# A paired feed-forward on one Trainium2 core: second products taken one token tile at a time in two PSUM banks, attention scores made three tiles at a time in six

## The chip, the cores and the metric

The kernel runs on one core of one Trainium2 chip. The metric is the device time of one execution in microseconds (us). The engines have short names here, as in the profile: PE is TensorE, the matrix unit, and PEld its weight loads; DVE is VectorE, ACT is ScalarE, POOL is GpSimd, and SP only issues DMAs. Each engine works through its own instructions in the order in which the program emits them, and waits on semaphores where another engine has to be done first. PSUM, where PE leaves its results, has eight banks of 512 fp32 columns.

## The reference

Grouped attention over 8 samples of 384 tokens (16 query heads, 4 key heads, 64 columns a head), and then a feed-forward block on its output `x` (384 x 1024 per sample):

```
scores = q @ k^T / 8 ; attn = softmax(scores) ; x = attn @ v
a1  = alpha1 * x + beta1
u   = x + lam * (w_tok @ a1)            # mixes tokens, 384 x 384
a2  = alpha2 * u + beta2
out = u + lam * (relu(a2 @ w_ch1) @ w_ch2)   # 1024 -> 4096 -> 1024
```

## The kernel before, in words

**Samples.** Samples 0 and 1 go through a plain feed-forward (`main`). Samples 2 to 7 go in three pairs (`pair(i)`, samples 2+2i and 3+2i), and a pair's two large products are done with seven block products in place of eight; the sums that this needs are made by DVE. Attention for later samples is woven between the feed-forward matmuls: `main(0)` carries sample 1, `main(1)` carries 2 and 3, the second phase of pair 0 carries samples 4 and 5, that of pair 1 carries 6 and 7, and pair 2 carries none.

**A pair has two phases.** In the first (L693 to L738) PE makes the hidden layer: 8 groups of 14 blocks, each of 4 matmuls on 384 columns, into tiles that the code calls X, Y and Z. In the second (L739 to L796) it makes the output: seven products `o`, in the order 1, 2, 6, 5, 3, 7, 4, each of 3 token tiles `ms` by 16 hidden tiles `t`, so 48 matmuls on 512 columns into tiles called C. The 16 are cut in two halves `h`, and the three token tiles take turns within a half: three banks stay open. Sums over products are left to PSUM: a product that starts anew has `start` at its first matmul (only 1, 6 and 7), and the next products add to what lies there. After a half with h = 1 a C tile is evacuated: a copy by ACT (product 1), an add by DVE (6, 5, 3, 7, 4) or a multiplication by lam (2). For 3, 7 and 4 a multiplication by lam follows through `flush`, and a store by a POOL DMA.

**Units.** The generator stops (`yield`) every 4 second-product matmuls. One such step is called a unit here; a product has 12 and the phase has 84, numbered from 0. A table says what of attention is emitted after which unit (`put` at L450 and L932, `put_all(ps, 1, side(c)[1])` at L969 for the pair's first sample, and the same with 36 added for its second, L972). The entries per sample are:

- S, a block of scores: `scores2` (L303) makes two tiles of 1024 scores each, by 4 matmuls with 64 rows a tile, and ACT turns each tile to exponentials (L289). 18 tiles make a sample, so there are nine blocks, at units 0, 4, 8, ... 32.
- A (`av`, L410): 18 matmuls of attention times v for two heads; then DVE does a reciprocal, a multiplication that frees the PSUM tile (L328) and two operations for a1 (L333, L335). At units 7, 11, ... 35.
- T (`tok`, L341): 9 matmuls with w_tok; then DVE adds (L352), which frees the tile, and multiplies (L356), which makes a2. At units 10, 14, ... 38. Two units later a2 is spilled and turned by a DMA transpose (`flip`).
- turn (L429), only for head pairs 5 to 7 of the pair's second sample: PE transposes a2 instead, in 3 matmuls. At units 33, 36 and 40, so with 36 added 69, 72 and 76, each 2 units or more after its T.

**Other DVE work of the second phase.** `sums_a` (L590, 3 small operations each) at units 75, 75, 76 and 78 combines a2 for the next pair; `sum_w1` (L622) at the start of three (h, ms) blocks of product 4; and four "hidden sums" in each of products 2 and 6 (L788 to L794) of 0.95 us.

**PSUM in the pairs.** Pool `sc` gives tiles of two banks, two of them in turn: S, T and turn take one each, and so do the Y tiles. Pool `acc` gives three single banks: X, every second Z, and C. Pool `one` is a single bank: A and the other Z. A new tile of a pool takes the place of the oldest, and its first matmul waits until the last reader of that one is done.

**Weights of the second products** come as 28 blocks of 512 KB per pair, fetched by SP into a ring of 6 slots that the first-phase weights use too. `free` (L645) gives a slot back after its last matmul and starts one more load of the queue. The last two blocks of a pair go to `pad`, where there is room for two.

Of the kernel before, what the change touches and what calls it, by code (L numbers as in the profile page):

```python
# [12 lines left out]
def kernel(  # L13
# [182 lines left out]
    def three():  # L196
        if pairs:
            return pairs["sc"].tile([P, 2, 4, P], f32, tag="sc", name="sc", bufs=2)
        return threes[0].tile([P, 2, 4, P], f32, tag="sc", name="sc", bufs=3)

    def one():
        if pairs:
            return pairs["one"].tile([P, 4, P], f32, tag="one", name="one", bufs=1)
        return three()[:, 0]
# [25 lines left out]
    def side(b):  # L230
# [71 lines left out]

        def scores2(i):  # L303
            for k in range(2):
                scores(2 * i + k)
# [130 lines left out]
        if not first:  # L436


            turns = {}
            if b == 1:  # L440
                turns = {4: [(to_all, 3, 0, 0), (to_all, 3, 1, 1), (load_row_set, 1, 1, 0), (load_row_set, 2, 0, 1)],
                         8: [(k_transpose, 0)], 12: [(to_all, 1, 0, 2), (to_all, 1, 1, 0), (load_row_set, 2, 1, 0)],
                         16: [(scale_beta,)], 20: [(to_all, 2, 0, 1), (to_all, 2, 1, 0)],
                         24: [(q_transpose, 0, 2, "av")], 28: [(k_transpose, 2)]}
                for i in range(3):
                    turns[32 + 4 * i] = [(q_transpose, 2 + 2 * i, 2, "av")]
            if (b - NPL) // 2 > 0:
                at = {}

                def put(k, *m):  # L450
                    at.setdefault(k, []).append(m)

                for j in range(9):
                    put(4 * j, scores2, j)
                for p in range(NP):
                    put(4 * (p + 1) + 3, av, p)
                    put(4 * (p + 1) + 6, tok, p)
                    put(4 * (p + 1) + 8, flip, p)
                    if by_pe(p):
                        put(4 * (p + 1) + 8 + (p == NP - 3), turn, p)  # L460
                return turns, at
            return turns, {
                0: [(scores3, 0)], 4: [(av, 0)], 6: [(scores3, 1)], 8: [(tok_flip, 0)], 11: [(av, 1)],
                13: [(scores3, 2, True)], 15: [(av, 2)], 16: [(tok_flip, 1)], 18: [(tok_flip, 2)], 19: [(av, 3)],
                21: [(scores3, 3)], 23: [(tok_flip, 3)], 25: [(av, 4)], 27: [(scores3, 4)], 29: [(tok_flip, 4)],
                31: [(av, 5)], 33: [(scores3, 5, True)], 35: [(av, 6), (tok_flip, 5)], 37: [(av, 7)],
                38: [(tok_flip, 6)], 41: [(tok_flip, 7)],
                **{39 + 4 * i - i // 2 * 2: [(turn, p)] for i, p in enumerate((5, 6, 7)) if by_pe(p)}}
# [167 lines left out]
    def fetch(i, n, at=None):  # L636
        if at is None:
            w2_slots[i, n] = w1_free.pop(0)
            at = ring[:, w2_slots[i, n]]
        else:  # L640
            w2_slots[i, n] = None
        w2_at[i, n] = at
        nc.sync.dma_start(out=at, in_=w2s[n])

    def free(slot):  # L645
        if slot is None:
            return
        w1_free.append(slot)
        if queue:
            f, *a = queue.pop(0)  # L650
            f(*a)

    queue = [m for i in range(NB) for m in [(load_w1, c) for c in order1[2 if i else RING:]]
             + [(fetch, i, n) for n in range(SLOTS - 2 if i + 1 < NB else SLOTS)] + [(load_w1, c) for c in order1[:2] if i + 1 < NB]]
# [6 lines left out]
    def pair(i):  # L661
# [5 lines left out]
        def begin_end(ms):  # L667
            ends[ms] = t = piece().bitcast(f32)
            nc.sync.dma_start(out=t, in_=by_tok(out[b0 + 1])[:, ms, :512])
# [5 lines left out]
        def scaled(o, b, ms, dw, t):  # L675
            if o != 2:
                tt(out=t, in0=t, in1=lam_t[:, dw * 512:(dw + 1) * 512], op=MUL)  # L677
            store(b, ms, dw, t)
# [9 lines left out]

        def finish(ts):
# [3 lines left out]
        for g in range(NH // 2):  # L693
            X, Y, snap = {}, {}, {}
            for k, (o, e) in enumerate(SEQ1):
                t = 2 * g + e
                lo, hi = bias1[:, t:t + 1], bias1[:, NH + t:NH + t + 1]
                if o == 1:
                    X[e] = acc.tile([P, 512], f32, tag="acc", name="X", bufs=3)
                if o == 7:  # L700
                    Y[e] = pairs["sc"].tile([P, 2, 512], f32, tag="sc", name="Y", bufs=2)[:, 0]
                if o == 2:
                    Z = acc.tile([P, 512], f32, tag="acc", name="Z", bufs=3) if e else pairs["one"].tile(
                        [P, 512], f32, tag="one", name="Z", bufs=1)
# [35 lines left out]
        X = [[(0, 512, acc.tile([P, 512], f32, tag="acc", name="C", bufs=3))] for _ in range(NST)]  # L740
        snap = {}
        where = {2: (0, 0), 3: (0, 1), 7: (1, 1), 4: (1, 0)}
        for k, o in enumerate(PLACE2):
            for h in range(2):
                for ms in range(NST):
                    if o == 4 and not last and 1 < 3 * h + ms < 5:
                        sum_w1(0, (5, 7, 6)[3 * h + ms - 2])
                    if o == 5 and not last and h and ms < 2:
                        fetch(i, SLOTS - 2 + ms, pad[:, (1 + ms) * 2048:(2 + ms) * 2048])
                    if last and (o, h) in ((6, 1), (7, 0)):  # L750
                        (lift_end if o == 7 else begin_end)(ms)
                    if last and (o, h, ms) == (7, 0, NST - 1):
                        X[ms] = [(c0, c1, pairs["sc"].tile([P, 2, 512], f32, tag="sc", name="C", bufs=2)[:, 0, :c1 - c0])
                                 for c0, c1 in ((0, 384), (384, 512))]
                    for (c0, c1, x), t in ((c, t) for c in X[ms] for t in range(8 * h, 8 * h + 8)):
# [3 lines left out]
                                         start=(o in (1, 6, 7) and t == 0), stop=(t == NH - 1), skip_group_check=True)  # L759
                        if t % 4 == 3 and ms == NST - 1 and c1 == 512:  # L760
                            free(slot)
# [5 lines left out]
                        if t % 8 == 3 and c1 == 512:  # L767
                            flush(1)
                            yield 1
                    if h == 1 and not (last and o == 4):  # L770
# [6 lines left out]
                        for c0, c1, x in X[ms]:  # L777
                            if o == 1:
                                nc.scalar.copy(out=snap[o, ms], in_=x)
                            elif o in (6, 5):  # L780
                                tt(out=snap[o, ms], in0=x, in1=snap[1, ms], op=ADD)
                            elif o == 2:
                                tt(out=t, in0=x, in1=lam_t[:, :512], op=MUL)
                            else:
                                tt(out=t[:, c0:c1], in0=x, in1=snap[{3: 1, 7: 5, 4: 6}[o], ms][:, c0:c1], op=ADD)
                        if o not in (1, 6, 5):
                            later.append((scaled, o, b0 + bb, ms, dw, t))
                    if o in (2, 6) and (h, ms) in ((0, 1), (0, 2), (1, 0), (1, 1)):  # L788
                        r = [(0, 1), (0, 2), (1, 0), (1, 1)].index((h, ms))
                        ts = slice(4 * r, 4 * r + 4)  # L790
                        if o == 2:
                            tt(out=hid[:, ts, 0], in0=hid[:, ts, 3], in1=hid[:, ts, 0], op=SUB)
                        else:
                            tt(out=hid[:, ts, 4], in0=hid[:, ts, 4], in1=hid[:, ts, 0], op=SUB)  # L794
# [5 lines left out]
    with tc.manual_schedule(engines=order):  # L800
# [162 lines left out]
        for i in range(NB - 1):  # L963
# [6 lines left out]
            for u, f, h in ((10, flip_q, 0), (17, flip_k, 0), (18, flip_q, 2), (25, flip_q, 4), (33, flip_k, 2), (33, flip_q, 6)):  # L970
                put(ps, 1, u, f, c + 1, h, 2)
            put_all(ps, 1, side(c + 1)[1], lambda u: u + 36)  # L972
            for j, u in ((1, 75), (0, 75), (2, 76), (3, 78)):
                put(ps, 1, u, sums_a, j)
        for ps in range(NPL + NB):
# [8 lines left out]
            if ps == NPL - 1:  # L984
                side_banks.close()
                mm_banks.close()
                for name in ("sc", "acc", "one"):
# [33 lines left out]
```

## Time and profile before

| what | us |
|---|---|
| three runs | 743.80, 743.89, 745.25 (median 743.89) |
| the profiled execution, its own time | 745.27 |
| its span, first to last instruction | 743.5 |
| PE idle before an instruction, longest: at the very start, then anywhere later | 1.52, 0.60 |

By stage (the view of busy time by stretch), in us; the two second phases that carry attention are in the fourth and sixth row:

| stretch | length | PE busy | DVE busy | ACT busy |
|---|---|---|---|---|
| `main(1)`, first phase, 130.9 to 190.1 | 59.2 | 57.46 | 40.94 | 22.34 |
| `main(1)`, second phase, to 244.2 | 54.1 | 53.48 | 38.24 | 18.78 |
| pair 0, first phase, to 316.9 | 72.7 | 72.70 | 63.10 | 48.38 |
| pair 0, second phase, to 418.9 | 102.0 | 101.05 | 74.91 | 38.33 |
| pair 1, first phase, to 491.8 | 72.9 | 72.90 | 56.38 | 48.42 |
| pair 1, second phase, to 593.7 | 101.9 | 100.95 | 74.82 | 38.28 |
| pair 2, first phase, to 666.7 | 73.0 | 73.00 | 56.00 | 48.47 |
| pair 2, second phase and end, to 743.5 | 76.8 | 72.42 | 31.76 | 2.11 |

How to read it: a line of the timeline has the start, the time from the start of its first instruction to the end of its last, the engine, the line of the code, the operation, `out<-in` by tile names, the shape, and how many instructions were merged; a bracket at the end is the idle time of that engine ahead of it and what ended it. Matmuls overlap, so the time that a block takes on PE is read from start to start of two blocks, not from its length. A few matmul records are missing from the trace: where a group shows x7 or x3, it had 8 or 4.

### The profile page before, as it was taken

The page shows a single profiled execution, that of the slowest core. Times are in us where ns is not written, and L with a number is a line of the kernel's source. Part 1 is how long each engine was busy: PE and PEld are TensorE (multiplying, and loading weights), DVE is VectorE, ACT ScalarE, POOL GpSimd, SP SyncE. Part 2 cuts the span into 40 slices and gives each one's busy share as a digit, 9 for nine tenths or more (in the row PEclk, how much of TensorE's full clock was granted, in tenths as well). Part 3 has the DMA queues.
Part 4 walks back from the last instruction along what each step waited for, and adds up shares of the span by engine and source line. Part 5 has one row for each costly group of instructions (what it writes and reads, how often), then busy time and mean ns, then how long its engine had stood idle before and what let it go on. Part 6 is the DMA issues. An engine that isn't in the chain of part 4 may idle for free.

```text
span 743.5 us, 14441 instructions
## 1 busy us (share of the span) xinstructions
PE 731.1 (98%) x5708; PEld 416.1 (56%) x5769; DVE 514.6 (69%) x998; ACT 319.3 (43%) x458; POOL 163.4 (22%) x211
## 2 busy tenths in 40 slices
PE   8999999999999999999999999999999999999997
PEld 5866555566555566645555566655555566654444
DVE  7763366567687889748778977747957987762354
ACT  7632431334332566653443366664334166660000
POOL 9434220420000232201003433210002331000011
PEclk9999999999999999999999999999999999999999
DMA  9999999999998999999979999998988998935976
GB/s 185 194 201 200 207 219 168 172 184 204 221 275 243 178 222 214 256 219 213 272 246 205 200 174 174 173 216 181 246 278 221 183 165 115 162 117 176 291 210 158
DMA packets 218017, 151.32 MB, mean 204 GB/s; under 512 B 88660, under 2 KB 197060, under 8 KB 217948
## 3 DMA queue, kind: packets, MB, share of 16 engines
q0 software_dynamic: 120304, 64.60, 65.8%
q1 hardware_dynamic: 97100, 85.39, 42.3%
q8 instruction: 45, 0.74, 0.4%
q10 hardware_dynamic: 544, 0.39, 0.2%
q14 instruction: 24, 0.20, 0.1%
HBM read 154.84 MB, written 38.27 MB: 260 GB/s over the span
## 4 chain that ended last, share of the span: by engine, by line
PE 85%; DMA 8%; POOL 2%; issue 2%; DVE 2%; POOLq 0%; DVEq 0%
PE C L757 29%; PE X L707 17%; PE Y L707 8%; PE ch L575 8%; PE h L537 7%; PE Z L707 4%; PE sc L280 4%; PE sc L345 3%; DMA ops<-a 3%; DMA w<-in_moe_w_ch_dram 2%; PE one L320 2%; DMA q_raw<-in_q_dram 2%; PE sc L320 1%; POOL w L185 1%; DMA rows<-in_moe_lam_dram 1%
## 5 line engine op out<-in xcount | busy, mean ns | idle before, releaser
L757 PE MATMUL C<-w,arena 128*128 128x512 bf16 (+2 forms) x949 | 219.9, 372 | 2.3
L289 ACT ACTIVATE es<-sc 128x1024 bf16<-128x1024 f32 x126 | 121.8, 1022 | 162.7 <-PE sc L280 158.6
L757 PEld LDWEIGHTS <-arena 128*128 128x128 bf16 x1040 | 93.7, 98 | 99.8 <-issue 7.6
L712 ACT ACTIVATE hT<-X,bias 128x384 f32<-128x384 f32 x144 | 83.7, 581 | 67.4 <-PE X L707 60.4
L707 PEld LDWEIGHTS <-w 128*128 128x128 bf16 x768 | 75.1, 98 | 50.3 <-issue 0.4
L185 POOL DMA_DIRECT2D w<-in_moe_w_ch_dram x68 | 62.4, 924 | 128.9 <-PE X L707 68.2
L575 PE MATMUL ch<-arena,hT 128*128 128x512 bf16 x366 | 87.9, 379 | 1.0 <-issue 0.3
L522 POOL DMA_DIRECT2D out_dram<-hT x33 | 29.3, 887 | 261.5 <-DVE hT L677 135.7
L537 PE MATMUL h<-ops,w 128*128 128x384 bf16 (+1 forms) x480 | 83.7, 327 | 1.9 <-DVE hT L548 0.9
L707 PEld LDWEIGHTS <-pad 128*128 128x128 bf16 x576 | 56.4, 98 | 37.2
L707 PE MATMUL X<-ops,w 128*128 128x384 bf16 x384 | 70.5, 326 | 0.0
L707 PE MATMUL X<-ops,pad 128*128 128x384 bf16 x384 | 70.3, 326 | 0.0
L537 PEld LDWEIGHTS <-w 128*128 128x128 bf16 x480 | 45.1, 98 | 32.3 <-issue 2.8
L575 PEld LDWEIGHTS <-hT 128*128 128x128 bf16 x384 | 34.7, 98 | 36.8 <-issue 2.5
L352 DVE TENSOR_TENSOR xr<-sc,xr 128x384 f32<-128x384 f32 x56 | 31.1, 555 | 34.1 <-PE sc L345 34.1
L320 PEld LDWEIGHTS <-es 128*128 128x128 bf16 x1008 | 38.3, 97 | 12.4
L280 PE MATMUL sc<-qT,kT 64*128 64x384 bf16 (+2 forms) x576 | 43.8, 272 | 0.9 <-DVE xr L328 0.2
L345 PEld LDWEIGHTS <-wtokT 128*128 128x128 bf16 x576 | 37.4, 98 | 12.9 <-DVE a L335 2.7
L707 PE MATMUL Z<-ops,w 128*128 128x384 bf16 x192 | 39.1, 326 | 0.0
L707 PE MATMUL Y<-ops,w 128*128 128x384 bf16 x192 | 39.1, 326 | 0.0
L714 DVE TENSOR_TENSOR arena<-Y,hT 128x384 bf16<-128x384 f32 x48 | 26.8, 558 | 17.3 <-ACT hT L712 15.0
L345 PE MATMUL sc<-a,wtokT 128*128 128x128 bf16 x504 | 37.3, 219 | 0.1
(140 smaller groups left out, 858.2 us busy)
## 6 DMA issues: line engine op xcount, KB each, us to landing
w<-w2s SPq DMA_DIRECT2D x80, 512.0 KB, 4.7
w<-in_moe_w_ch_dram POOLq DMA_DIRECT2D x68, 512.0 KB, 9.9
out_dram<-xr SPq DMA_DIRECT2D x56, 192.0 KB, 5.6
out_dram<-hT POOLq DMA_DIRECT2D x33, 256.0 KB, 6.9
arena<-in_moe_w_ch_dram POOLq DMA_DIRECT2D x16, 512.0 KB, 19.8
w2s<-arena SPq DMA_DIRECT2D x28, 256.0 KB, 3.5
q_raw<-in_q_dram POOLq DMA_DIRECT2D x28, 192.0 KB, 10.4
w2s<-pad SPq DMA_DIRECT2D x16, 256.0 KB, 2.7
```

The source lines that it names most:

```text
L185: nc.gpsimd.dma_start(out=w1[:, w1_slots[c]], in_=w1src[:, :, c * CW * P:(c + 1) * CW * P])
L280: nc.tensor.matmul(out=sc[:, hh, k % 4:k % 4 + n], lhsT=kT[r, 2 * p // G, BLK[hh][sk], :], rhs=qT[r, p, st:st + n, :], start=True, stop=True)
L289: nc.scalar.activation(out=e, in_=sc, func=EXP, scale=scale_qk)
L320: nc.tensor.matmul(out=av[:, hh, sq, :], lhsT=ess[k // 4][:, m % 2, k % 4, :], rhs=vb[:, sk, hk, :], start=(sk == 0), stop=(sk == NST - 1))
L345: nc.tensor.matmul(out=ps[:, tt, :], lhsT=wtokT[:, st, tt * P:(tt + 1) * P], rhs=a1s[p][:, st, :], start=(st == 0), stop=(st == NST - 1 an ...
L352: nc.vector.tensor_tensor(out=u, in0=ps, in1=u, op=ADD)
L522: nc.gpsimd.dma_start(out=at, in_=o, accum_op=ADD)
L537: nc.tensor.matmul(out=ps[:, :n], lhsT=w1[:, w1_slots[c], dt, j * P:(j + 1) * P], rhs=a2T[:, dt, :n], start=(dt == 0), stop=(dt == NDT - 1))
L575: nc.tensor.matmul(out=ps, lhsT=hT[:, nt, ms * P:(ms + 1) * P], rhs=w2[:, row(nt)[0], row(nt)[1], cs], start=(i == 0), stop=(i == NNT - 1))
L707: nc.tensor.matmul(out=ps, lhsT=tb[g, o][:, dt, e * P:(e + 1) * P], rhs=opb(LEFT1[o])[:, dt], start=(o in (1, 2, 7) and dt == 0), stop=(dt ...
L712: nc.scalar.activation(out=snap[o, e], in_=ps, func=IDENT, bias=hi if o == 5 else lo)
L757: nc.tensor.matmul(out=x, lhsT=hid[:, t, LEFT2[o], ms * P:(ms + 1) * P], rhs=rhs[:, t % 4 * 512 + c0:t % 4 * 512 + c1], start=(o in (1, 6, ...
```

## The change

**Second products.** In pairs 0 and 1 all products but the last (4) run token tile by token tile: all 16 hidden tiles for one `ms`, then the next. Every product now starts anew in PSUM (`start` at its first matmul), so only two C banks are open in turn, and the sums over products that PSUM held are added when a tile is evacuated: product 2 becomes an add and a multiplication by lam, and product 7 has a second add that builds the base for product 4. That is 6 more DVE operations on 512 columns in a phase. The four hidden sums of products 2 and 6 move to other units (third, sixth, ninth and eleventh of the product). A unit is still 4 matmuls, and the phase still has 84.

**PSUM.** `sc` now gives three tiles of two banks and `acc` two single banks; `one` is gone. A takes an `sc` tile. X of the first phase becomes one `sc` tile for both halves of a group, and so does Y; Z is in `acc`. In product 4, which keeps its halves, the C tile of the third `ms` is taken from `sc`.

**Attention table of samples 4 to 7.** S makes three tiles in a block (six blocks a sample, as samples 2 and 3 already have). The units are:

| | before | after |
|---|---|---|
| S | 0, 4, 8, ... 32 (two tiles) | 0, 6, 12, 20, 25, 30 (three tiles) |
| A | 7, 11, ... 35 | 4, 10, 14, 18, 23, 28, 32, 34 |
| T | 10, 14, ... 38, its `flip` two later | 8, 15, 17, 22, 27, 33, 36, 39, with its `flip` |
| turn (second sample) | 33, 36, 40 | 36, 38, 40 |
| added for the second sample | 36 | 37 |
| `sums_a` | 75, 75, 76, 78 | 76, 76, 77, 79 |

**Weights.** Blocks 6, 7, 14, 15, 22, 23, 26 and 27 go to the two places in `pad`, the others to the ring; the loads keep one queue, whose head waits for a place of its kind. A block is now given back only in the third token tile of a product. Of the next pair's first-phase weights two loads are queued ahead of blocks 26 and 27, and two behind.

**Pair 2** keeps its halves and its accumulation in PSUM; only its tiles come from other pools, and three tiles for its end lie elsewhere.

The core of the diff:

```diff
     def three():
         if pairs:
-            return pairs["sc"].tile([P, 2, 4, P], f32, tag="sc", name="sc", bufs=2)
+            return pairs["sc"].tile([P, 2, 4, P], f32, tag="sc", name="sc", bufs=3)
...
     def one():
-        if pairs:
-            return pairs["one"].tile([P, 4, P], f32, tag="one", name="one", bufs=1)
         return three()[:, 0]
...
-                for j in range(9):
-                    put(4 * j, scores2, j)
+                for j in range(6):
+                    put((0, 6, 12, 20, 25, 30)[j], scores3, j, j in (2, 5))
                 for p in range(NP):
-                    put(4 * (p + 1) + 3, av, p)
-                    put(4 * (p + 1) + 6, tok, p)
-                    put(4 * (p + 1) + 8, flip, p)
+                    put((4, 10, 14, 18, 23, 28, 32, 34)[p], av, p)
+                    put((8, 15, 17, 22, 27, 33, 36, 39)[p], tok_flip, p)
                     if by_pe(p):
-                        put(4 * (p + 1) + 8 + (p == NP - 3), turn, p)
+                        put((36, 38, 40)[p - NP + 3], turn, p)
...
         def scaled(o, b, ms, dw, t):
-            if o != 2:
+            if o != 2 or not last:
                 tt(out=t, in0=t, in1=lam_t[:, dw * 512:(dw + 1) * 512], op=MUL)
...
                 if o == 1:
-                    X[e] = acc.tile([P, 512], f32, tag="acc", name="X", bufs=3)
+                    if not e:
+                        both_x = pairs["sc"].tile([P, 2, 512], f32, tag="sc", name="X", bufs=3)
+                    X[e] = both_x[:, e]
...
-        X = [[(0, 512, acc.tile([P, 512], f32, tag="acc", name="C", bufs=3))] for _ in range(NST)]
+        def c_banks(ms):
+            return [(0, 512, pairs["sc"].tile([P, 2, 512], f32, tag="sc", name="C", bufs=3)[:, 0] if ms == NST - 1 else
+                     acc.tile([P, 512], f32, tag="acc", name="C", bufs=2))]
+
+        X = [c_banks(ms) if last else None for ms in range(NST)]
...
-            for h in range(2):
+            whole = not last and o != 4
+            for h in range(1 if whole else 2):
                 for ms in range(NST):
...
+                    if whole:
+                        X[ms] = [(0, 512, acc.tile([P, 512], f32, tag="acc", name="C", bufs=2))]
+                    elif not last and h == 0:
+                        X[ms] = c_banks(ms)
+                    upto = NH if whole else 8 * h + 8
...
-                                         start=(o in (1, 6, 7) and t == 0), stop=(t == NH - 1), skip_group_check=True)
+                                         start=((not last or o in (1, 6, 7)) and t == 0), stop=(t == NH - 1),
+                                         skip_group_check=True)
...
-                        if t % 8 == 3 and c1 == 512:
-                            flush(1)
+                        if t % 4 == 3 and t < upto - 1 and c1 == 512:
+                            q = 4 * ms + t // 4
+                            if whole and o in (2, 6) and q in (2, 5, 8, 10):
+                                sums_hid(o, (2, 5, 8, 10).index(q))
+                            if t % 8 == 3:
+                                flush(1)
                             yield 1
...
+                                base = {2: 1, 3: 1 if last else 5, 7: 5, 4: 6}[o]
+                                tt(out=t[:, c0:c1], in0=x, in1=snap[base, ms][:, c0:c1], op=ADD)
+                            if o == 7 and not last:
+                                tt(out=snap[6, ms], in0=x, in1=snap[6, ms], op=ADD)
...
-            for j, u in ((1, 75), (0, 75), (2, 76), (3, 78)):
+            put_all(ps, 1, side(c + 1)[1], lambda u: u + 37)
+            for j, u in ((1, 76), (0, 76), (2, 77), (3, 79)):
                 put(ps, 1, u, sums_a, j)
...
-                for name in ("sc", "acc", "one"):
+                for name in ("sc", "acc"):
                     pairs[name] = ST(tc.psum_pool(name=name, bufs=3))
```

## Prediction

> **What bounds the kernel now.** I read the page's first part, then the busy time by stretch, then PE's timeline in the stretch that changes, and last DVE's.
>
> ```profile
> PE 731.1 (98%) x5708; PEld 416.1 (56%) x5769; DVE 514.6 (69%) x998; ACT 319.3 (43%) x458; POOL 163.4 (22%) x211
> ```
>
> PE bounds it everywhere. In the second phases of pairs 0 and 1 it is busy for 101.05 of 102.0 and 100.95 of 101.9 us, and nothing there waits for DVE, ACT or a DMA. PE's instructions stay the same in number and size, so there is no wait to remove. What can be won is what PE loses at a change of the kind of matmul, and what can be lost is any new wait, of which there is none to start from. PE's timeline, first a block of two score tiles in pair 0, then one of three tiles in `main(1)`:
>
> ```profile
> 402.27 1.02 PE L757 MATMUL C<-w,arena 128*128 128x512 bf16 x4
> 403.23 0.61 PE L280 MATMUL sc<-qT,kT 64*128 64x256 bf16 x8
> 403.77 1.04 PE L757 MATMUL C<-w,arena 128*128 128x512 bf16 x4
> ...
> 194.41 1.89 PE L575 MATMUL ch<-arena,hT 128*128 128x512 bf16 x7
> 196.23 0.83 PE L280 MATMUL sc<-qT,kT 64*128 64x384 bf16 x12
> 196.99 1.90 PE L575 MATMUL ch<-arena,hT 128*128 128x512 bf16 x8
> ```
>
> Start to start, 4 C matmuls take 0.865 (1.73 for 8 elsewhere), but 0.96 ahead of scores: 0.095 is lost going in. Two tiles take 0.54 and three 0.76, so a tile is 0.22 and 0.10 more is lost coming out. A block costs 0.20 beside its tiles. By the same reading A is 0.55, T 0.50, a turn 0.165, and a unit q = 0.865.
>
> **What is gained.** Nine score blocks become six per sample: 3 x 4 samples x 0.20 = 2.4 us less PE time. The trace has a second reading of it: PEld idles ahead of its loads for scores, 59 times with no releaser.
>
> ```profile
> PEld L280 <- issue: 23.4, 59, 0.4
> ```
>
> [...]
>
> **What DVE gets.** Six more operations on 512 columns in a phase, and the queue's order. Its prices, from its queue in pair 1 where it never idles:
>
> ```profile
> 514.88 0.56 DVE L352 TENSOR_TENSOR xr<-sc,xr 128x384 f32<-128x384 f32 x1 [0.39 <-PE sc L345]
> 515.47 0.56 DVE L356 TENSOR_TENSOR obuf<-xr,vecs 128x384 bf16<-128x384 f32 x1
> 515.95 0.68 DVE L783 TENSOR_TENSOR hT<-C,vecs 128x512 f32<-128x512 f32 x1
> 516.54 0.95 DVE L792 TENSOR_TENSOR arena<-arena 128x1536 bf16<-128x1536 bf16 x1
> 517.41 0.19 DVE L325 RECIPROCAL rinv<-one 128x6 f32<-128x6 f32 x1
> 517.64 0.56 DVE L328 TENSOR_TENSOR xr<-one,rinv 128x384 f32<-128x384 f32 x1
> 518.23 0.56 DVE L333 TENSOR_TENSOR a1f<-xr,vecs 128x384 f32<-128x384 f32 x1
> 518.82 0.56 DVE L335 TENSOR_TENSOR a<-a1f,vecs 128x384 bf16<-128x384 f32 x1
> 519.30 0.68 DVE L783 TENSOR_TENSOR hT<-C,vecs 128x512 f32<-128x512 f32 x1
> ```
>
> From start to start: T 1.07 (its tile free after 0.56, a2 after 1.15), an evacuation E or a multiplication by lam M 0.60, a hidden sum 0.87, A 1.89 (its tile free after 0.79). DVE starts 0.74 after PE starts an A, 0.70 after a T. Six operations are 3.6 us on 74.9 of 101.9: it fits on average, so whether it costs is a matter of places. I went through all entries of the new table, with E, M and hidden sums in emission order, and asked at each PE entry whether its PSUM tile (the third allocation before it in `sc`) and its input are ready. That such a wait falls on the third tile of a block, and for what, `main(0)` shows where DVE was late:
>
> ```profile
> 107.80 0.61 PE L280 MATMUL sc<-qT,kT 64*128 64x384 bf16 x8
> 108.65 0.39 PE L280 MATMUL sc<-qT,kT 64*128 64x128 bf16 x4 [0.24 <-DVE xr L328]
> ```
>
> Four places fail in each of the two pairs:
>
> (a) Unit 25, third tile, needs A of unit 23. DVE works without a pause from A of unit 14: 0.74, then A, E, T, M, sum, T, A, E, sum, M, sum, T, E and 0.79, together 14.1 after that A started on PE. PE gets there after 4.53 of attention and 11 q, 14.05. Wait 0.1.
>
> (b) Unit 37, the second sample's first block. Its third tile needs T of unit 36, one unit before. From the start of A at unit 32, DVE: 0.74, A 1.89, T 1.07, sum 0.87, A 1.89, E 0.60, 0.56 = 7.6. PE: A, T, A, T 2.10, 5 q 4.33, and 0.52 in the block = 6.95. Wait 0.7.
>
> (c) Unit 75, the second turn, needs a2 of T at unit 73. From A at unit 69, DVE: 0.74, A, T, two E (product 7 now has two), A, M, 1.15 = 8.5. PE: A, T, A, turn, T 2.27 and 6 q 5.19 = 7.45. Wait 1.1.
>
> (d) The end of the phase. T is now at unit 76, two later, and its turn at 77. T starts 0.70 after PE, a2 needs 1.15, and PE is at the turn after 0.50 + q = 1.37: wait 0.5 whatever DVE has queued. Then comes the larger part. The C tile of the third `ms` of product 4 is an `sc` tile, T and turn take the next two, and the third is X, the next pair's first tile. So the first matmul of the next phase waits for the last evacuation (L785), and before the change it didn't:
>
> ```profile
> 585.34 0.67 PE L345 MATMUL sc<-a,wtokT 128*128 128x128 bf16 x9
> ...
> 593.78 1.60 PE L707 MATMUL X<-ops,w 128*128 128x384 bf16 x8
> ...
> 586.04 0.56 DVE L352 TENSOR_TENSOR xr<-sc,xr 128x384 f32<-128x384 f32 x1 [0.44 <-PE sc L345]
> ...
> 595.16 0.68 DVE L785 TENSOR_TENSOR hT<-C,hT 128x512 f32<-128x512 f32 x1
> ```
>
> There the last T goes to PE at 585.34, X starts 8.44 later, and the last evacuation ends at 595.84, 2.06 after X has started: DVE has four groups of `sums_a`, three `sum_w1`, three E and three M to do. In the new order one `sum_w1` (0.60) moves ahead of T, so from T's start on DVE to the end of that evacuation it is 9.80 - 0.60 = 9.2. X can start 0.70 + 9.2 + 0.07 for the signal = 9.97 after T starts on PE. Without waits it would be 8.44 less two units, 6.71. PE loses 3.26 in all, 0.5 at the turn and 2.7 ahead of X.
>
> (e) Once, at the start of pair 0: X now lies in the first banks, where I take `main(1)`'s last two tiles to be. DVE ends the last of these (L582) at 245.12; X starts at 244.23 now. With the signal the wait is 0.96 if the tile as a whole waits, 0.3 if only its second half does, and 0 if it lies elsewhere. I take 0.96, as a tile is one thing to wait for, and keep 0.
>
> Behind a waiting matmul stands all of PE, which sets the end, so each wait counts in full; the first phases after it are PE's alone (no PE idle before L707) and give nothing back.
>
> **What costs nothing.** With two C banks a bank has 16 matmuls, 3.5 us, between its last matmul and its next first, and the attention between them, as before between halves; the latest evacuation, at unit 35, ends 2.9 after its matmul by the chain of (b), and its bank is wanted 4 units and 1.05 of attention on, 4.5. A's tiles, five and six entries on, are free otherwise. Exponentials: three take 2.85, and the A that needs the third comes 4 units later, 3.5. Weight blocks: between a slot's last matmul and the new block's first there are now 15 units against 12, and a fetch lands in 4.7; of blocks 26 and 27 the last is asked for after unit 71 and used in 79. If that cover is gone, the price is the rest of a 4.7 fetch, twice. SP's queue holds the spill of one T ahead of it, and POOL has the same stores, six of them one M later. Pair 2 has no attention and room for DVE (31.76 of 76.8): nothing.
>
> **Sum.** Against the profiled execution's 745.27: -2.4 + 0.96 + 2 x (0.1 + 0.7 + 1.1 + 3.26) = +8.9, so 754.2. The median of the runs is 743.89, 1.38 lower; the same step gives 752.8.
>
> [...]
>
> **Rivals.** *Only the end waits.* The chains of (b) and (c) are sums of six or seven rows and lose if DVE is ahead by one operation; (d) rests on one stretch of the trace. Then 2 x 3.26 + 0.3 - 2.4 = +4.4: 748.3. *DVE isn't behind at the end either:* then X still waits for the last evacuation, 0.16 for PE's end, 0.69 and 0.07 = 0.9, and the turn 0.5; 2 x 1.4 - 2.4 = +0.4: 744.3, no change. For it speaks only that DVE's share of the phase stays under 80%; against it that before the change DVE was already 2.06 late there. *Faster:* X gets a tile that is free, not C's, and turns and third tiles find DVE done. Its price is the whole gain, 741.5. It decides where DVE's chain from the last T is under 6 us in place of 9.2; the row at 595.16 speaks against it, and so does the wait in `main(0)`, where the third allocation is what is waited for. *The scores aren't made three at a time:* where the third tile waits, a block falls in two, as at 107.80, and loses its 0.20 too; with (a) and (b) that is 4 of 24 blocks, under 1 us. *Dearer:* a late weight block, or chains one more operation behind in (b) to (d), 2 x 3 x 0.6 = 3.6: 756.
>
> **Chances.** Forecast (750 to 755) 0.62; only the end 0.16; no change 0.06; faster 0.09; dearer 0.07. What a measurement of this kernel can tell from no change is about 0.2%, 1.5 us. The range 746 to 757.5 leaves out faster, no change and the far ends, under 0.2. Faster by over 0.2%: 0.09; within: 0.06; slower: 0.85.
>
> **What would show it.** PE idle before L707 X of about 2.7 us, released by DVE L785, at the start of pairs 1 and 2; PE idle before L432 (the turns) of 1.1 and 0.5, released by DVE or by the copy it waits for; before L280, some 0.7, by DVE L352; before the first X of pair 0, by L582. Score blocks of 0.76 in both pairs, and a second phase of 100.7 us were it not for the waits. I am wrong if X starts at once, if PE stays at 98% in these phases, or if a DMA of `w2s` ends a wait.

## The result, and the profile after

| | us |
|---|---|
| before, median of 6 runs | 744.13 |
| after, median of 6 runs (877.13 to 882.12) | 880.37 |
| ratio, 95% interval | 1.1823 [1.1800, 1.1847] |
| the profiled execution after, its own time; its span | 882.12; 880.3 |

The forecast of 752.8 and its range to 757.5 were far too low. The sign was right, but for most of the loss the cause was another.

The first part of the page after:

```profile
PE 766.7 (87%) x5769; PEld 418.3 (48%) x5769; DVE 522.8 (59%) x1010; ACT 319.4 (36%) x458; POOL 163.5 (19%) x211
```

PE has the same matmuls and is no longer busy for 98% but for 87%. So PE stands still, and the stage lengths say where. They are taken from PE's timeline, from the first matmul of a phase to the first of the next, in us:

| stretch | before | after | difference |
|---|---|---|---|
| up to pair 0 | 244.23 | 243.92 | -0.31 |
| pair 0, first phase | 72.80 | 116.75 | +43.95 |
| pair 0, second phase | 101.91 | 102.79 | +0.88 |
| pair 1, first phase | 72.94 | 115.19 | +42.25 |
| pair 1, second phase | 101.90 | 105.79 | +3.89 |
| pair 2, first phase | 72.94 | 115.20 | +42.26 |
| pair 2, second phase and end | 76.78 | 80.66 | +3.88 |

Of 136.8 us, 128.5 lie in the three first phases. The prediction worked on the second phases and moved only the start of the first ones. PE's waits after, as engine, line, tile and what was waited for, then us in total, times and the longest:

```profile
PE X L716 <- ACT hT L721: 51.8, 73, 0.7
PE Y L716 <- DVE arena L729: 25.5, 24, 1.7
PE X L716 <- ACT arena L727: 16.1, 24, 0.7
PE sc L426 <- DVE obuf L350: 4.2, 3, 2.9
PE C L774 <- DMA pad<-w2s: 2.3, 1, 2.3
```

There are three pairs of eight groups, so 24 groups, and each has five of the first three kinds of wait: four ahead of an X block, one ahead of a Y block (one group of pair 0 has one more). These three lines make 93.4 us, less than was lost, since a wait leaves out two things that start-to-start times hold: a block without a wait starts 0.16 before the one ahead of it is done, and some blocks start late without any idle time. One group in PE's timeline after (pair 1, its first blocks and its two blocks of product 4):

```profile
463.46 0.81 PE L716 MATMUL X<-ops,w 128*128 128x384 bf16 x4
464.94 0.81 PE L716 MATMUL X<-ops,w 128*128 128x384 bf16 x4 [0.67 <-ACT hT L721]
465.59 0.81 PE L716 MATMUL Y<-ops,w 128*128 128x384 bf16 x4
466.42 0.81 PE L716 MATMUL X<-ops,pad 128*128 128x384 bf16 x4
...
475.12 0.81 PE L716 MATMUL Y<-ops,pad 128*128 128x384 bf16 x4
476.99 0.81 PE L716 MATMUL Y<-ops,pad 128*128 128x384 bf16 x4 [1.06 <-DVE arena L729]
```

And beside it ACT's reads of the first two X blocks, and DVE's read of the first of the two Y blocks with the operation ahead of it:

```profile
464.31 0.58 ACT L721 ACTIVATE hT<-X,bias 128x384 f32<-128x384 f32 x1 [5.35 <-PE X L716]
465.79 0.58 ACT L721 ACTIVATE hT<-X,bias 128x384 f32<-128x384 f32 x1 [0.90 <-PE X L716]
...
475.79 0.68 DVE L624 TENSOR_TENSOR pad<-w,pad 128x1024 bf16<-128x1024 bf16 x1
476.39 0.55 DVE L729 TENSOR_TENSOR arena<-Y,hT 128x384 bf16<-128x384 f32 x1
```

A block that follows without a wait starts 0.65 after the one before it (464.94 to 465.59). The second X block starts 1.48 after the first. It writes the other half of the joined X tile, in the other bank, and it needs nothing that ACT makes. Still it starts only when ACT has read the first half: block end 464.27, ACT from 464.31 to 464.89, X at 464.94. So 0.83 is lost. After the Y block in between, the next X block starts 0.83 after it in place of 0.65, since ACT is then reading the second half: 0.18 more. In product 4 the second Y block waits for DVE's read of the first: 1.87 in place of 0.65, 1.22 lost. Some 0.4 of it is DVE's own lateness: it is still busy with a weight sum (L624) when the first Y block is done, and in the last group of each phase, which has no such sum there, the wait is 0.65 in place of 1.06. Per group that is 4 x 0.83 + 3 x 0.18 + 1.22 = 5.08, and 24 groups make 122. From the third group on the waits for L721 read 0.73 where they were 0.67, and the group takes 14.54 in place of 14.18; 18 such groups are 6.5 more, together 128.4. (The shorter last groups, 1.2 us in all, and longer waits in pair 0 about cancel.) The waits grow because ACT starts its read 0.91 after the block's start in place of 0.85; the read itself still takes 0.58. Why it starts later isn't known.

The places in the second phase that the prediction named, in PE's timeline after: (b), and the two turns of (c) and (d).

```profile
406.78 0.61 PE L278 MATMUL sc<-qT,kT 64*128 64x384 bf16 x8
407.96 0.39 PE L278 MATMUL sc<-qT,kT 64*128 64x128 bf16 x4 [0.57 <-DVE xr L346]
...
455.14 0.34 PE L426 MATMUL sc<-ident,obuf 128*128 128x128 bf16 x3 [0.97 <-DVE obuf L350]
...
458.10 0.34 PE L426 MATMUL sc<-ident,obuf 128*128 128x128 bf16 x3 [0.38 <-DVE obuf L350]
```

And DVE's operation for the last T, and its last evacuation of the phase:

```profile
456.89 0.56 DVE L346 TENSOR_TENSOR xr<-sc,xr 128x384 f32<-128x384 f32 x1 [1.20 <-PE sc L339]
...
465.40 0.68 DVE L811 TENSOR_TENSOR hT<-C,hT 128x512 f32<-128x512 f32 x1
```

The third score tile and the turns wait as forecast. The next phase's X at 463.46 doesn't: it starts 1.94 before this evacuation does.

### The profile page after: what moved, and what is told of

Same layout as the page of the kernel before. It is cut to its first block, busy times and chain, and to the rows that moved or that the text cites. A ratio compares the mean times of both kernels' runs of the same rounds, so it can differ in the third digit from the quotient of the medians.

```text
span 880.3 us, 14519 instructions
## 1 busy us (share of the span) xinstructions
PE 766.7 (87%) x5769; PEld 418.3 (48%) x5769; DVE 522.8 (59%) x1010; ACT 319.4 (36%) x458; POOL 163.5 (19%) x211
## 4 chain that ended last, share of the span: by engine, by line
PE 70%; ACT 10%; DVE 9%; DMA 5%; issue 3%; POOL 2%; ACTq 0%; SPq 0%; DVEq 0%; POOLq 0%
PE C L774 22%; PE X L716 17%; ACT hT L721 8%; PE ch L568 8%; PE h L530 8%; PE sc L278 3%; PE Y L716 3%; PE sc L314 3%; PE sc L339 2%; PE Z L716 2%; DMA q_raw<-in_q_dram 2%; ACT arena L727 2%; DVE pad L624 1%; DVE arena L729 1%; DMA out_dram<-xr 1%
## 5 line engine op out<-in xcount | busy, mean ns | idle before, releaser
L774 PE MATMUL C<-w,arena 128*128 128x512 bf16 (+2 forms) x736 | 169.4, 376 | 0.0
L774 PEld LDWEIGHTS <-arena 128*128 128x128 bf16 x1040 | 95.5, 98 | 104.6 <-issue 10.5
L721 ACT ACTIVATE hT<-X,bias 128x384 f32<-128x384 f32 x144 | 83.7, 581 | 166.8 <-PE X L716 163.9
L716 PE MATMUL X<-ops,pad 128*128 128x384 bf16 x384 | 77.8, 324 | 37.4 <-ACT hT L721 34.3
L716 PE MATMUL X<-ops,w 128*128 128x384 bf16 x384 | 77.9, 324 | 35.9 <-ACT hT L721 17.5
L568 PE MATMUL ch<-arena,hT 128*128 128x512 bf16 x384 | 90.8, 379 | 0.0
L774 PE MATMUL C<-pad,arena 128*128 128x512 bf16 (+2 forms) x304 | 69.7, 375 | 2.3 <-DMA pad<-w2s 2.3
L716 PE MATMUL Y<-ops,pad 128*128 128x384 bf16 x192 | 39.0, 325 | 25.5 <-DVE arena L729 25.5
L725 DVE TENSOR_TENSOR arena<-Z,hT 128x384 bf16<-128x384 f32 x48 | 26.5, 552 | 31.8 <-PE Z L716 31.8
```

Source lines behind the costliest of these rows:

```text
L568: nc.tensor.matmul(out=ps, lhsT=hT[:, nt, ms * P:(ms + 1) * P], rhs=w2[:, row(nt)[0], row(nt)[1], cs], start=(i == 0), stop=(i == NNT - 1))
L716: nc.tensor.matmul(out=ps, lhsT=tb[g, o][:, dt, e * P:(e + 1) * P], rhs=opb(LEFT1[o])[:, dt], start=(o in (1, 2, 7) and dt == 0), stop=(dt ...
L721: nc.scalar.activation(out=snap[o, e], in_=ps, func=IDENT, bias=hi if o == 5 else lo)
L774: nc.tensor.matmul(out=x, lhsT=hid[:, t, LEFT2[o], ms * P:(ms + 1) * P], rhs=rhs[:, t % 4 * 512 + c0:t % 4 * 512 + c1], start=((not last o ...
```

## The experiments

**Theory A:** a PSUM tile is waited for as a whole, so two halves of a joined tile that are written and read in turn run one after the other. **Rival B:** something else in the change slows the first phase: the two `acc` banks in place of three, the order of the weight loads, or reads and writes in neighbouring banks. **Rival C:** three `sc` tiles are too few for X and Y to take turns in.

**x_y_apart.** After, with X and Y as single tiles again and the two Z joined in their place:

```diff
-                    if not e:
-                        both_x = pairs["sc"].tile([P, 2, 512], f32, tag="sc", name="X", bufs=3)
-                    X[e] = both_x[:, e]
+                    X[e] = acc.tile([P, 512], f32, tag="acc", name="X", bufs=2)
...
-                        both_y = pairs["sc"].tile([P, 2, 512], f32, tag="sc", name="Y", bufs=3)
-                    Y[e] = both_y[:, e]
+                    Y[e] = pairs["sc"].tile([P, 2, 512], f32, tag="sc", name="Y", bufs=3)[:, 0]
...
-                    Z = acc.tile([P, 512], f32, tag="acc", name="Z", bufs=2)
+                    if not e:
+                        both_z = pairs["sc"].tile([P, 2, 512], f32, tag="sc", name="Z", bufs=3)
+                    Z = both_z[:, e]
```

> The changed kernel, but with every half of X and of Y in a tile of its own: X in the two single banks, Y in two sc tiles, and Z's two halves in one sc tile instead. Theory A (a tile is waited for as a whole: a write into one half waits until the last reader of the other half is done): the first phases fall back from 116.8, 115.2 and 115.2 us to 73 each, no wait of PE for L721, L727 or L729 is left, and the time is 744.1 + 0.9 + 3.9 + 3.9 (what the trace shows lost in the other stretches) = 752 to 753. Rival B (the chip lets ACT read and PE write two neighbouring banks only in turn): X's halves still lie in two neighbouring banks, so the X waits stay and the time is 840 or more. Rival C (three sc tiles are too few for X and Y to rotate): now two Y and a Z rotate through the same three, so the waits stay, 850 or more.

Measured: 753.17 (median of 4), ratio 1.0132 [1.0092, 1.0173]; its profiled run 750.92. The first phases are 74.81, 73.51 and 73.51, so 125.3 of the 128.5 us are gone. Its PE waits:

```profile
PE sc L426 <- DVE obuf L350: 2.7, 4, 1.0
PE C L772 <- DMA pad<-w2s: 1.7, 1, 1.7
PE Z L714 <- DVE arena L723: 1.5, 3, 0.7
...
PE sc L278 <- DVE xr L346: 1.2, 2, 0.6
PE X L714 <- DVE hT L809: 1.1, 2, 0.6
```

None of them lies between two halves of X or of Y. The first and the fourth are at the table's places. The second is a late weight block in pair 2. In the third the two Z blocks now share a tile and DVE is late with the first, in pair 0. The last is an X block behind an evacuation, at the start of pairs 1 and 2. The two `acc` banks and the new order of the loads are still there, and two Y and a Z now take turns in the three `sc` tiles, yet the phases are within 0.6 to 2.0 us of before: B and C are out as the main cause. X's two halves lie in the two `acc` banks; whether these are neighbours isn't shown.

**y_joined and x_joined.** The two halves of that edit, each alone: in the first only X is taken apart, in the second only Y (the two Z joined as in x_y_apart in the first, in single banks as in after in the second).

> The changed kernel with only X apart (in the two single banks); Y stays one tile for both halves, Z is one sc tile. Theory A: only the second block of product 4 waits, 1.22 us more from start to start in each of 24 groups, 29 us: 780 to 784, with PE waiting for DVE L729's line alone. Rival B: X and Y wait as before, about 880. Rival C: about 880.

> The changed kernel with only Y apart (two sc tiles); X stays one tile, Z in the single banks. Theory A: per group four X blocks start 0.83 late and three more 0.18 late, 3.86 us, times 24 is 93: 843 to 848. Rival B: the same or more than 880 minus the Y part, 850. Rival C: above 880, since three tiles now serve one more.

Measured, one run each: 782.93 and 851.23. Against x_y_apart's profiled 750.92, Y joined costs 32.0 (24 x 1.22 = 29.3, and its late weight blocks wait 1.7 longer) and X joined 100.3. The first is in the range expected, the second 3 us over it; the growth of the waits from 0.67 to 0.73 was not in that sum. The two together are 132.3, about the 131.2 that lie between x_y_apart's profiled run and after's, so the two costs add up.

**before_x_joined.** The kernel before with nothing of the change but the joined X (Y then takes `acc`):

```diff
-                    X[e] = acc.tile([P, 512], f32, tag="acc", name="X", bufs=3)
+                    if not e:
+                        both_x = pairs["sc"].tile([P, 2, 512], f32, tag="sc", name="X", bufs=2)
+                    X[e] = both_x[:, e]
...
-                    Y[e] = pairs["sc"].tile([P, 2, 512], f32, tag="sc", name="Y", bufs=2)[:, 0]
+                    Y[e] = acc.tile([P, 512], f32, tag="acc", name="Y", bufs=3)
```

> The kernel before with one part of the change alone: X's two halves in one sc tile of two banks (two such tiles in turn), Y in the single banks that X had. Nothing of attention, second products or weights is changed. Theory A: 24 x 3.86 = 93 us more, 835 to 840. A rival that blames the new attention table, the second products or the pools' sizes: 744.

Measured, in one run: 844.28, 100.4 over before's 743.89: the same price as in the kernel after, and 4 us over the range expected, as in x_joined. Its two longest PE waits:

```profile
PE X L709 <- ACT hT L714: 51.8, 73, 0.7
PE X L709 <- ACT arena L720: 16.0, 24, 0.7
```

The same counts and lengths as after: this part of the change alone, in a kernel that has none of the rest, makes the X waits. Here only X uses the joined tiles in this phase and takes turns in two of them, so the waits need no Y or Z beside X in the pool (C).

**other_order.** After, with tiles joined as they are, and the blocks of a group in another order, so that a block on the other tile lies between most halves:

```diff
-    SEQ1 = ((1, 0), (1, 1), (7, 0), (6, 0), (6, 1), (7, 1), (5, 0), (5, 1), (2, 0), (3, 0), (3, 1), (2, 1), (4, 0), (4, 1))
+    SEQ1 = ((1, 0), (7, 0), (1, 1), (7, 1), (6, 0), (2, 0), (6, 1), (2, 1), (5, 0), (5, 1), (3, 0), (4, 0), (3, 1), (4, 1))
```

> The changed kernel with X and Y still in one tile each, only the order of the 14 blocks of a group in the first phase is another: 1a 7a 1b 7b 6a 2a 6b 2b 5a 5b 3a 4a 3b 4b (a and b the halves), so that most pairs of X blocks have a block of another tile between them. Theory A: a block in between (0.65 us) covers 0.65 of the 0.83 by which an X block starts late, so five X blocks lose 0.18, two lose 0.83, one Y block 0.57: 3.1 us a group in place of 5.1, 24 groups: 832 to 840. A rival in which each of the 120 handovers costs a fixed time, or the banks collide: 880, unchanged.

Measured, in one run: 818.33, 14 us under the range expected. The wait lines fall to one, two a group:

```profile
PE X L716 <- ACT hT L721: 34.5, 48, 1.0
```

Two are left where X blocks follow each other (5, 5, 3). A Y or Z block between two X blocks covers the rest of the read but for some 0.2. A group loses (818.33 - 750.92) / 24 = 2.81 against x_y_apart's profiled run: two of 0.83 and some five of 0.2. The direction and the place of the X waits were as expected. The Y wait of 0.57 a group, 13.7 us in all, did not come: an X block now lies between the two Y blocks of product 4 and no PE wait for DVE is left there. That is about the whole miss. The run excludes a fixed price for each handover, which would have left the time at 880. It does not tell the tile from the banks, since a block in between would hide either. Against the banks speak two other things: x_y_apart, as far as its two `acc` banks are neighbours, and the kind of the wait, for the profile, which infers what ends a wait from semaphore events, names the read of the other half. That points to a wait that the program places, not to a slower write.

**apart_ring and apart_table.** From here on the question was what else costs, with x_y_apart as the base. apart_ring sends the last two weight blocks of pair 2 to the ring in place of `pad`. apart_table changes DVE's order and the table: turns at 36, 40 and 42, `sums_a` at 76, 76, 78 and 81, the later two hidden sums of product 6 moved into product 5, the multiplications by lam of product 4 put off to its end, and the third `sum_w1` one block later.

> The kernel with X and Y apart (Z in one sc tile), and in pair 2 the weight blocks 26 and 27 in the ring in place of pad. Theory: in pair 2 the places in pad come free 24 matmuls, 5.2 us, ahead of their next use, about what a fetch takes, so PE waits for the fetch; in the ring they are asked for a product earlier. The wait of PE for a weight DMA (1.7 to 3.4 us in the kernels so far) is gone and pair 2's second phase with the end is 76.8 us in place of 78.4; the rest is as with X and Y apart, 749 to 751. Rival (the DMA engines are simply too busy at the end): the wait stays.

> The kernel with X and Y apart, and only DVE's order in the second phases of pairs 0 and 1 changed: the two later hidden sums of product 6 go into product 5, the turns go to units 36, 40 and 42 of the table, sums_a to 76, 76, 78 and 81, in product 4 the multiplications by lam wait until its end and the third sum_w1 goes one block later. The prediction's points (b), (c) and (d): PE's waits ahead of L278 (0.58), the turns (0.97 and 0.38) and X (0.55) go, and these phases are 100.7 to 101.0 us in place of 102.8, the first phases after them 73.0 in place of 73.5: 746 to 748 with the fetch at the end still late. If those waits had another cause than DVE's order, the phases stay at 102.8.

Measured, one run each: 749.0 and 749.38. The runs of x_y_apart differ by more than that among themselves (750.32 to 756.28), so the waits and the stage lengths tell more here than the time. In apart_ring the wait of 1.7 at the end is gone and the last stretch is 76.57, as before the change (76.78). In apart_table the waits ahead of turns, scores and X are gone, but there are three waits for weight blocks in `pad`, 4.7 us together, where there was one of 1.7: the time is 1.4 to 3.4 over what was expected. PE came earlier to blocks whose loads started no earlier: in pair 0 it was ready for block 27 at 413.74, 7.0 after SP issued its load (406.73), and got it 8.7 after; in x_y_apart it came to this block 8.7 after the issue.

**v2 and v3.** v2 puts these together: X and Y apart, the table, pair 2's last blocks in the ring, S of unit 25 at 26, the second Z block one place later, four `xr` buffers in place of three and one `a1f` in place of two. v3 changes one line of v2:

```diff
-    PADDED = (6, 7, 14, 15, 22, 23, SLOTS - 2, SLOTS - 1)
+    PADDED = (4, 5, 12, 13, 20, 21, SLOTS - 2, SLOTS - 1)
```

> All of it together: X and Y apart, the ring for the last two blocks, DVE's new order, the score block of unit 25 at 26, the second half of product 2 of the first phase one block later (so that the shared Z tile has been read), and four buffers for xr in place of three (one for a1f in place of two). What should be left of the change is 12 score blocks less and no wait: 744.1 - 2.4 = 741.7, so 741.5 to 743, a ratio of 0.997 to 0.9985. If DVE's six extra operations per phase cost in some place that I have not seen, 744 to 747.

> The version v2 with one thing changed: in a pair the two places in pad hold blocks 4, 5, 12, 13, 20, 21 (the first two of each second product of a couple) in place of 6, 7, 14, 15, 22, 23 (the last two), and 26, 27 as before. Its PE waits of v2 were two, both for late weight blocks 26 (1.64 us at 414.29 and 2.13 us at 589.64). Blocks 20 and 21 are used up two units before 22 and 23, so the places come free 2 x 0.865 = 1.7 us earlier at the least, and the loads of 26 and 27 stand ahead of the spill of the T at unit 70 in SP's queue rather than behind it. Theory: the lateness is only the time at which a place comes free; then both waits go or fall to under 0.4 us, and with the clock loss behind the second of them v3 takes 743.97 - 2.4 + 0.5 = 741 to 742.5, ratio 0.996 to 0.998. Rival: the fetch is late because the DMA engines are busy or the queue is held by another load ahead; then waits of 1.5 us and more stay and v3 takes 743.5 to 744.5 as v2.

Measured: v2 744.10 (median of 11), ratio 1.0008 [0.9990, 1.0026], no difference, and above what was expected. One kind of PE wait of the change was left in its profiled run, once in each of pairs 0 and 1:

```profile
PE C L775 <- DMA pad<-w2s: 3.8, 2, 2.1
```

v3 took 740.57 (median of 6) against 744.16, ratio 0.9951 [0.9939, 0.9963]: faster than the kernel before. That wait is gone; the longest that PE has left, at the start and in `main`, are in stages that the change doesn't touch:

```profile
PE warm L830 <- DVE wtokT L833: 1.5, 1, 1.5
PE h L530 <- DVE hT L541: 1.0, 2, 0.7
```

Its second phases take 100.52 and 100.26 against 101.91 and 101.90. So without its waits the change, with six score blocks in place of nine, is worth 3.0 us there, somewhat more than the 2.4 predicted for the blocks alone. Its first phases, 73.02, 72.80 and 72.80, are as before. The edit cured the lateness. It lets the places in `pad` come free two units earlier; it also puts the two loads ahead of one spill in SP's queue, and which of the two did it was not told apart.

## Why the prediction was wrong, point by point

**The step that failed** is the sentence that "the first phases after it are PE's alone (no PE idle before L707) and give nothing back". It asks only whether a first phase gives time back, and takes it as otherwise unchanged. The description of the change says that X and Y become one tile for both halves, and point (e) even said that "a tile is one thing to wait for". But the sum has no term for it inside the phase. That term is worth 128.5 of the 136.8 us: PE writes the second half of a joined tile only after ACT or DVE has read the first, five times in each of 24 groups.

Most of it could have been had from the rows of before: an X block starts 0.65 after the one ahead of it and lasts 0.81, and ACT's read of 384 columns takes 0.58. With signals of 0.04 and 0.05, as after shows them, a second half starts 1.48 later. With DVE's part, read from after, that gives the 122 us of the sum above, and a forecast near 875. "No PE idle before L707" was the view that misled: it shows that the kernel before has no wait there, with tiles that are apart.

**The predicted points,** in us; the lateness is read from start to start:

| point | predicted | after, in pair 0 |
|---|---|---|
| gain per score block of 12 matmuls | 0.76 long, 0.20 saved | 0.76 long |
| (a) unit 25 | 0.1 | 0.10 |
| (b) unit 37 | 0.7 | 0.75 |
| (c) unit 75, turn | 1.1 | 1.12 |
| (d) unit 77, turn | 0.5 | 0.55 |
| (d) X after the last evacuation | 2.7 | 0 |
| (e) start of pair 0 | 0.96 | 0.79 |
| weight blocks | 0 | 0; in pair 2 3.9 with the clock |

Points (a) to (c) and the turn of (d) were right in mechanism and size. Pair 0's second phase should have come to -1.2 + 2.4 = +1.2 without the wait ahead of X, and came to +0.88. Of "what costs nothing", the C banks and the exponentials held: no wait for either is in the list.

**(d), the wait ahead of X,** failed at the step "T and turn take the next two, and the third is X". DVE's chain came as computed: T's operation starts at 456.89 and the evacuation ends at 466.08, 9.19 for the predicted 9.2. But X did not get C's tile, since it runs while that one is still to be read. It got one that was free by then, the likeliest being that of the T or the turn, whose last reader was done; a new tile then doesn't always take the place that was handed out longest ago, as the prediction and the description of the pools had it. Which rule chooses it was not tried. In x_y_apart, where X lies in `acc`, X's second half does wait for an evacuation (0.55 at the start of pairs 1 and 2).

**"What costs nothing"** failed for the weight blocks. The prediction took 4.7 for a fetch, the median of before. After, the load of block 27 of pair 2 stands in the chain that ended last with 8.04, and PE waited 2.25 for it:

```profile
862.24 8.04 DMA pad<-w2s
...
870.32 6.18 PE L774 MATMUL C<-pad,arena 128*128 128x512 bf16 x28 [2.25 <-DMA pad<-w2s]
```

For pair 2 the prediction looked at attention and DVE alone. There the products keep their halves, and the places in `pad` come free only at the end of product 7, 5.2 before PE comes to block 26. apart_ring shows the price without the clock, about 1.8. In pairs 0 and 1 such waits came when others were removed, in apart_table and v2, until v3 moved the loads forward. The prediction named a late `w2s` as what would make it wrong, and it did, in a few us.

**In pair 1's second phase** (+3.89) one turn waited 2.86. DVE stood for 1.94 of it ahead of L322, for the spill that still held the `xr` buffer:

```profile
675.02 0.34 PE L426 MATMUL sc<-ident,obuf 128*128 128x128 bf16 x3 [2.86 <-DVE obuf L350]
...
671.56 0.56 DVE L322 TENSOR_TENSOR xr<-sc,rinv 128x384 f32<-128x384 f32 x1 [1.94 <-DMA out_dram<-xr]
```

That had not been looked at. In x_y_apart, with other times, it didn't occur, and the phase was +0.88.

**That 753.17 of x_y_apart is close to the forecast of 752.8** is mostly chance: it has 1.1 of the wait ahead of X (5.4 in the sum) and nothing of (e), but late Z and a late weight block in their place, and two of its four runs show a lower mean clock (0.995 and 0.998) and are 5 us longer than the others.

**The gain per score block** held: after the change 4 C matmuls ahead of a score block still take 0.96 (405.82 to 406.78), and a block of three tiles 0.76 (385.20 to 385.96).

**The clock.** The longest waits of PE cost granted clock as well, for which the sum has no term. The columns that matter here are the first, the stretch, and the third from the end, the granted clock. After, behind the waits of 2.86 and 2.25:

```profile
676.00:678.00 2.00, 2.00 (x14) 1.27 (x12) 0.58 (x2) 0.00 (x0) 0.90 (x1) 0.50 1.28 248
...
871.00:874.00 3.00, 3.00 (x9) 1.10 (x8) 1.39 (x2) 0.00 (x0) 0.00 (x0) 0.51 0.00 0
```

In x_y_apart, behind a wait of 1.70:

```profile
742.00:744.00 2.00, 2.00 (x12) 0.98 (x11) 1.66 (x3) 0.00 (x0) 0.00 (x0) 1.00 0.00 0
```

The shortest wait behind which the clock fell, of 2.07 in other_order, and the longest behind which it didn't, of 1.91 in x_joined, each with the stretches that follow:

```profile
806.14 6.18 PE L774 MATMUL C<-pad,arena 128*128 128x512 bf16 x28 [2.07 <-DMA pad<-w2s]
806.00:809.00 3.00, 2.86 (x8) 1.11 (x8) 1.22 (x2) 0.00 (x0) 0.00 (x0) 0.58 0.07 12
809.00:812.00 3.00, 3.00 (x19) 1.57 (x18) 1.51 (x4) 0.00 (x0) 0.00 (x0) 0.85 0.23 87
...
42.58 9.97 PE L530 MATMUL h<-ops,w 128*128 128x385 bf16 x60 [1.91 <-DVE hT L541]
42.00:44.00 2.00, 1.42 (x9) 0.90 (x10) 0.99 (x2) 0.00 (x0) 0.00 (x0) 1.00 1.42 198
44.00:46.00 2.00, 2.00 (x14) 1.17 (x12) 1.42 (x4) 0.56 (x2) 0.87 (x1) 1.00 1.45 199
```

The clock fell to half behind the five longest idle times of PE in these runs: 2.86 and 2.25 (after), 2.47 (apart_table), 2.13 (v2: 0.50 from 590 to 592, 0.70 from 592 to 594) and 2.07 (other_order). It stayed full behind the next shorter ones: 1.91 (x_joined), 1.70 (x_y_apart), 1.67 (after, 1.00 from 272 to 278) and 1.64 (v2) by the granted clock, 1.81 (y_joined) and 1.71 (apart_table) by the four C matmuls behind them, which take 1.02 as behind the 1.64. In after it is 3.4 us at half the clock each time (675.94 to 679.36 and 870.50 to 873.92, worked out from the granted clock of stretches of 0.5 and 1 us). In other_order 0.42 of 3 us and 0.15 of the next 3 are missing, 1.7 in all. Work shows the same: 28 C matmuls take 6.18 behind the waits of 2.25, 2.47 and 2.07, and 4.50 behind the 1.70, so some 1.7 us are lost each time. The predicted wait of 2.7 ahead of X lies among the lengths that cost clock here; had it come, it would by this estimate have cost some 1.7 us too.

## What to carry to other kernels

In these kernels a tile is the unit in which the program waits (X's halves in one tile: 844.28 in before_x_joined for 743.89 before). Before two buffers that are written and read in turn are joined into one, take the time from the first write's end through its reader to the next write, and multiply it by how often that happens. Go through every phase whose tiles a change touches, also those in which no instruction is added or moved, since a view with no waits in it tells only of the tiles as they were. And when a wait is removed on the engine that bounds, look for the load that is then late, and let its place come free earlier.

## What the runs showed of the hardware that was not expected

- The granted clock halved behind each PE gap of 2.07 to 2.86 us (five cases; for 3.4 us in the two of after), and not behind those of 1.64 to 1.91 (six cases). Over a first phase after, with gaps of 0.67 to 0.73 every few us, it was 1.00 (463.46 to 578.65).
- Going into and out of a score block costs 0.20 beside its tiles by PE's timeline (before: 0.96 in place of 0.865 ahead of it, and 0.54 for two tiles of 0.22). With twelve fewer blocks the second phases of v3 are 3.0 us shorter, 0.25 for each; the other 0.05 may come from other small changes of order and wasn't told apart.
- A weight load of 512 KB, in the median of before 4.7 into the ring (80 loads) and 6.3 into `pad` (4 loads), took 8.04 into `pad` in pair 2 after, asked for right behind another one (both issues within 1.41, from 861.82).
